# Moving five small transfers ahead of three transposes in a full DMA queue

The change: the transfers that put the last rows of a small matrix M in place go behind the third turned query tile instead of the sixth; the fourth to sixth turned query tiles follow them.

## The chip, the cores and the metric

One core of one Trainium2 chip. The metric is the device time of the whole kernel in microseconds (us).

Engines: PE is TensorE (PEld its weight loads), DVE VectorE, ACT ScalarE, POOL GpSimd, SP SyncE, whose queue SPq issues most of the DMA transfers here (93 of the 117 DMA instructions in the trace of before). All data matrices are bf16.

## The reference, cut to what matters

```python
def _A_ref(x, wqkv, wo):                      # S = 2048, D = 640, 32 heads of 20
    q, k, v = ...                             # from x @ wqkv
    phi = lambda t: jnp.where(t > 0, t + 1, jnp.exp(t)) + 1e-6
    pq, pk = phi(q), phi(k)
    kv = einsum(pk, v); z = sum(pk)
    o = (pq @ kv) / (pq @ z + 1e-6)
    return o @ wo
def _B_ref(x, w1, w2, w3, w4):
    h  = gelu(layernorm(x) @ w1)              # then shifted along the sequence, @ w2
    x1 = x + hs
    return x1 + gelu(layernorm(x1) @ w3) @ w4
return g * A + (1 - g) * B                    # g = sigmoid(x . gate_w)
```

The kernel folds `kv` and `wo` into one 640x640 matrix M, so the attention output of a 128-row tile is (normalized `pq` tile) @ M.

## The kernel before: the parts that matter

A scheduler written in Python orders the whole program when it is built. Work is a set of items; an item is emitted when the items it depends on have been emitted, and that fixes the order of each engine's instructions, with semaphores between engines. So a dependency added to an item can order a queue without any data behind it. The items here:

```python
def m_first():                       # matmuls for most of M; ACT and DVE evict them to M_sb
    ...
def m_tail():                        # item ("mt",): the last rows of M, into rows 60..67 of M_sb
    for j in range(KD):              # KD = 5
        sch.dma("sp", M_sb[60:68, j, :], Mt[8 * j:8 * j + 8, :], "mt", group_total=KD)
def qt_tile(t):                      # item ("qt", t): turn a normalized query tile
    sch.dma("sp", pqnT[:, :, 128 * t:128 * (t + 1)], pq_tok[:, t, :], ..., transpose=True)
def t_xn(which, t):                  # item ("t2", t): turn a layernormed tile
    sch.dma("sp", xnT[:, :, 128 * t:128 * (t + 1)], xn[:, sx, :], ..., transpose=True)
def a_tile(t):                       # item ("a", t): attention output of tile t
    ts(pool, abx[:, sa, :], x_tok[:, t, :], stg[:, 3, t:t + 1], ...)          # GpSimd
    mm_group(..., [(pqnT[:, j, tok], M_sb[:, j, 0:512]) for j in range(KD)])  # PE
    mm_group(..., [(pqnT[:, j, tok], M_sb[:, j, 512:D]) for j in range(KD)])
    stt(abx[:, sa, :], psf[...], stg[:, 2, t:t + 1], abx[:, sa, :], ...)      # DVE evicts
# ... cut ...
IT.add("MT", ("mt",), 0.0, m_tail, deps=[(("m", 1), 1.5), (("qt", 5), 0.0)])
IT.add("T2", ("t2", u), 0.0, lambda u=u: t_xn(2, u), deps=[(("n2", u), 1.1)] + ([(("mt",), 0.0)] if u == 12 else []))
IT.add("QT", ("qt", t), 0.0, lambda t=t: qt_tile(t), deps=[..., (("t2", 11 if t < 6 else NT - 1), 0.0)])
IT.add("AT", ("a", t), 1.33, lambda t=t: a_tile(t), deps=[(("qt", t), 3.0), ..., (("mt",), 2.5), ...])
```

The order on SP is therefore: xn tiles 8 to 11, query tiles 0 to 5, the five M transfers, xn tiles 12 to 15, query tiles 6 on. `xn` has three buffers, so GpSimd cannot normalize tile 15 before tile 12 has been turned. On PE the first attention tiles are interleaved with groups of the W3 matmul: a group, tile 0, a group, tile 1, and so on.

## Time and profile before

| | before |
|---|---|
| median, 3 runs | 262.55 us (262.35 to 262.55) |
| span in the profile | 261.4 us |
| PE busy | 257.3 us, 98% |
| PE wait for the M transfers | 0.78 us in the timeline, about 0.95 us of lost time (below) |

First part of the page of before (engine, busy us, share, instructions):

```profile
span 261.4 us, 4276 instructions
PE 257.3 (98%) x1665; PEld 133.9 (51%) x1665; DVE 151.7 (58%) x289; ACT 112.1 (43%) x241; POOL 93.0 (36%) x152
```

With PE busy for 257.3 of 261.4 us, a change that takes no work away can gain only from a gap on PE. The list of PE's waits in before has three lines (who waited, for whom, us in total, times, longest):

```profile
PE ps L848 <- POOL xn L660: 1.1, 1, 1.1
PE ps L601 <- DMA M_sb<-Mt: 0.8, 1, 0.8
PE ps L875 <- DMA wq<-in_A_wqkv_dram: 0.2, 1, 0.2
```

Only the second lies in the middle of the kernel. The SP queue's timeline around it, before (start us, us, what, count; in brackets idle time and releaser, where there is any):

```profile
120.69 5.79 SPq L281 DMA_TRANSPOSE xnT<-xn  x4
126.53 9.00 SPq L281 DMA_TRANSPOSE pqnT<-pq_tok  x6
135.66 4.13 SPq L285 DMA_DIRECT2D M_sb<-Mt  x5
139.88 5.19 SPq L281 DMA_TRANSPOSE xnT<-xn  x4
145.12 7.89 SPq L281 DMA_TRANSPOSE pqnT<-pq_tok  x6
```

PE's timeline in the same stretch, before:

```profile
126.45 0.74 PE L1006 MATMUL ps<-wo_aug,Lt 60*64 60x512 bf16 x16
127.12 13.12 PE L601 MATMUL ps<-xnT,w 128*128 128x512 bf16 x60
141.03 1.53 PE L601 MATMUL ps<-M_sb,pqnT 128*128 128x512 bf16 x10 [0.78 <-DMA M_sb<-Mt]
```

And the chain that ended last, before, in order of time:

```profile
127.19 10.91 PE ps L601 x50
138.13 0.61 ACT h2T L657
138.73 0.38 SPq L285
139.16 1.81 DMA M_sb<-Mt
141.03 9.92 PE ps L601 x60
```

How to read these: six transposes keep SP's queue until 135.53, the five M transfers are then issued one after the other until 139.79, and 0.06 us after the last of them has landed (139.16 + 1.81 = 140.97) the first attention matmul starts. The issue of the last transfer takes only 0.62 us; the chain counts the landing, 1.81 us after the issue starts. The ACT and SPq pieces of the chain are inferred releasers between the W3 matmuls and the issue; what stood ahead of that issue is read from the queue's own timeline.

Two more lines, GpSimd's and DVE's timelines of before, show what else was late there:

```profile
142.56 0.88 POOL L623 TENSOR_SCALAR xn<-x_tok,st 128x640 bf16<-128x640 bf16 x1 [11.63 <-DMA xnT<-xn]
144.33 0.88 DVE L640 SCALAR_TENSOR_TENSOR abx<-ps,stg,abx 128x640 f32<-128x640 f32 x1 [3.02 <-POOL abx L623]
```

GpSimd waited for xn tile 12 to be turned, and so DVE evicted the first attention tile late.

### The profile page before, as it was taken

The numbers are of one execution on the slowest core, as the hardware profiler recorded it, in microseconds if no ns is written. First come the engines' busy times: TensorE is split into PE (matmuls) and PEld (weight loads), VectorE is DVE, ScalarE is ACT, GpSimd is POOL, SyncE is SP. The second block draws the span as 40 slices with busy tenths as digits, with TensorE's granted clock in tenths as the row PEclk, the third lists the DMA queues.
The fourth block names the chain that finished last, engine by engine and source line by source line (L and its number), as shares of the span: only waits on it lengthen the run. The fifth ranks groups of instructions, "written<-read, shape, count | busy, mean of one in ns | idle before, by whom it ended". The sixth has DMA issues, their size and how long they took to land.

```text
span 261.4 us, 4276 instructions
## 1 busy us (share of the span) xinstructions
PE 257.3 (98%) x1665; PEld 133.9 (51%) x1665; DVE 151.7 (58%) x289; ACT 112.1 (43%) x241; POOL 93.0 (36%) x152
## 2 busy tenths in 40 slices
PE   8999999999999999999998999999999999999996
PEld 4655555554455555554444545654455644455453
DVE  1497787899903799998996406993023320133232
ACT  1386767759355766685853240005500035200000
POOL 4003996869864019667901401130011110021001
DMA  6865869582656991362572670123000020000211
GB/s 196 256 103 143 165 173 171 168 142 42 107 107 125 354 332 31 74 104 51 110 95 58 125 78 0 25 65 113 0 3 0 0 103 0 0 3 1 100 53 50
DMA packets 51348, 24.99 MB, mean 96 GB/s; under 512 B 42708, under 2 KB 49917, under 8 KB 51328
## 3 DMA queue, kind: packets, MB, share of 16 engines
q1 hardware_dynamic: 49952, 21.31, 35.4%
q0 software_dynamic: 1136, 3.28, 5.6%
q8 instruction: 13, 0.21, 0.3%
q10 hardware_dynamic: 240, 0.13, 0.2%
q14 instruction: 7, 0.06, 0.1%
HBM read 12.05 MB, written 2.62 MB: 56 GB/s over the span
## 4 chain that ended last, share of the span: by engine, by line
PE 96%; DMA 2%; SPq 0%; DVE 0%; ACT 0%; issue 0%
PE ps L601 60%; PE ps L1176 22%; PE ps L783 8%; PE ps L875 2%; DMA wq<-in_A_wqkv_dram 1%; PE ps L1088 1%; PE ps L1158 1%; DMA M_sb<-Mt 1%; PE ps L974 1%; PE ps L876 1%; SPq L285 0%; DVE x_tok L640 0%; PE ps L1006 0%; PE ps L612 0%; ACT h2T L657 0%; PE ps L1155 0%
## 5 line engine op out<-in xcount | busy, mean ns | idle before, releaser
L601 PE MATMUL ps<-xnT,w 128*128 128x512 bf16 x360 | 81.6, 379 | 0.0
L657 ACT ACTIVATE h2T<-ps 128x512 bf16<-128x512 f32 x52 | 30.5, 598 | 68.5 <-PE ps L601 68.5
L1176 PE MATMUL ps<-w,h2T 128*128 128x512 bf16 (+1 forms) x416 | 58.8, 299 | 0.0
L601 PEld LDWEIGHTS ps<-xnT,w 128*128 128x128 bf16 x360 | 34.2, 98 | 38.2 <-issue 0.9
L640 DVE SCALAR_TENSOR_TENSOR x_tok<-ps,stg,abx 128x512 bf16<-128x512 f32 (+1 forms) x32 | 17.3, 550 | 61.1 <-PE ps L1176 61.1
L623 POOL TENSOR_SCALAR abx<-x_tok,stg 128x640 f32<-128x640 bf16 x16 | 14.8, 928 | 97.5 <-DVE x_tok L640 94.2
L1176 PEld LDWEIGHTS ps<-w,h2T 128*128 128x128 bf16 x416 | 32.1, 98 | 24.9 <-issue 1.1
L623 POOL TENSOR_SCALAR xn<-x_tok,st 128x640 bf16<-128x640 bf16 x32 | 34.5, 1086 | 17.9 <-DMA xnT<-xn 17.2
L657 ACT ACTIVATE Er<-ps 128x640 bf16<-128x640 f32 x32 | 22.5, 705 | 18.5 <-PE ps L876 8.6
L601 PE MATMUL ps<-M_sb,pqnT 128*128 128x512 bf16 (+1 forms) x160 | 24.4, 299 | 0.8 <-DMA M_sb<-Mt 0.8
L656 ACT ACTIVATE junk<-x_tok 128x640 bf16<-128x640 bf16 x32 | 23.6, 737 | 3.1 <-DVE x_tok L638 2.6
L657 ACT ACTIVATE hsT<-ps 128x512 bf16<-128x512 f32 (+1 forms) x32 | 18.9, 593 | 13.4 <-PE ps L601 13.0
L601 PE MATMUL ps<-w,hsT 128*128 128x512 bf16 (+1 forms) x160 | 23.7, 299 | 0.0
L601 PE MATMUL ps<-wkg,xT 128*128 128x512 bf16 (+1 forms) x150 | 22.6, 299 | 0.0
L640 DVE SCALAR_TENSOR_TENSOR abx<-ps,stg,abx 128x640 f32<-128x640 f32 x16 | 14.1, 884 | 14.4 <-PE ps L601 7.4
L601 PEld LDWEIGHTS ps<-w,hsT 128*128 128x128 bf16 x160 | 13.3, 98 | 12.2
L601 PEld LDWEIGHTS ps<-M_sb,pqnT 128*128 128x128 bf16 x160 | 13.1, 98 | 11.9 <-DMA M_sb<-Mt 1.3
L601 PE MATMUL ps<-wq,xT 128*128 128x512 bf16 (+1 forms) x120 | 18.3, 299 | 0.0
L783 PE MATMUL ps<-pk_tok,x_tok 128*128 128x512 bf16 x80 | 17.8, 379 | 0.0
L623 DVE TENSOR_SCALAR Er<-Er 128x640 bf16<-128x640 bf16 x32 | 11.6, 362 | 9.4 <-ACT Er L657 9.2
L601 PEld LDWEIGHTS ps<-wkg,xT 128*128 128x128 bf16 x150 | 12.2, 97 | 9.0
L638 DVE SCALAR_TENSOR_TENSOR x_tok<-ps,x_tok 128x640 bf16<-128x640 f32 x16 | 13.1, 820 | 6.0 <-PE ps L601 5.1
(76 smaller groups left out, 241.1 us busy)
## 6 DMA issues: line engine op xcount, KB each, us to landing
w<-in_B_w_dram SPq DMA_DIRECT2D x1, 2160.0 KB, 8.2
w<-in_B_w_dram SPq DMA_DIRECT2D x1, 2080.0 KB, 15.1
x_tok<-in_A_x_dram SPq DMA_DIRECT2D x3, 640.0 KB, 5.7
out_dram<-x_tok SPq DMA_DIRECT2D x3, 640.0 KB, 3.1
w<-in_B_w_dram POOLq DMA_DIRECT2D x8, 160.0 KB, 4.4
wq<-in_A_wqkv_dram SPq DMA_DIRECT2D x5, 160.0 KB, 3.9
wkg<-in_A_wqkv_dram SPq DMA_DIRECT2D x5, 160.0 KB, 3.9
wv<-in_A_wqkv_dram POOLq DMA_DIRECT2D x1, 800.0 KB, 6.1
```

The costliest lines, as they stand in the source:

```text
L601: ins = e.matmul(out_ap, l, r, start=(i == 0), stop=(i == n - 1))
L623: return engf(lambda e: e.tensor_scalar(out_ap, in_ap, s1, s2, op0, op1), rd, [out_ap], cost=cost)
L638: return dve(lambda e: e.scalar_tensor_tensor(out_ap, in0, scalar, in1, op0, op1, accum_out=accum), rd, [out_ap, accum], cost=cost + 70.0)
L640: return dve(lambda e: e.scalar_tensor_tensor(out_ap, in0, scalar, in1, op0, op1), rd, [out_ap], cost=cost)
L656: return act(lambda e: e.activation(out_ap, in_ap, func, bias=bias, scale=scale, accum_out=accum), rd, wr, cost=cost)
L657: return act(lambda e: e.activation(out_ap, in_ap, func, bias=bias, scale=scale), rd, wr, cost=cost)
L783: ins = e.matmul(o, l, r, start=(t0 + q_ == 0), stop=(t0 + q_ == NT - 1))
L875: e.matmul(ps[:, b, 0:512], l, w[:, k, 0:512], start=(k == 0), stop=(k == KD - 1))
L876: return e.matmul(ps[:, b + 1, 0:n2], l, w[:, k, 512:512 + n2], start=(k == 0), stop=(k == KD - 1))
L974: ins = e.matmul(o, l, r_, start=st_, stop=sp_, skip_group_check=True)
L1088: ins = e.matmul(o, l, r, start=st, stop=sp)
L1176: ins = e.matmul(o, l, r, start=False, stop=(i == KFF - 1), skip_group_check=(n0 > 0))
```

## The change

Its intent: land the M rows before PE needs them, by letting three of the six query tiles wait behind them.

```diff
-    IT.add("MT", ("mt",), 0.0, m_tail, deps=[(("m", 1), 1.5), (("qt", 5), 0.0)])
+    IT.add("MT", ("mt",), 0.0, m_tail, deps=[(("m", 1), 1.5), (("qt", 2), 0.0)])
@@
-        IT.add("QT", ("qt", t), 0.0, lambda t=t: qt_tile(t), deps=[..., (("t2", 11 if t < 6 else NT - 1), 0.0)])
+        IT.add("QT", ("qt", t), 0.0, lambda t=t: qt_tile(t), deps=[..., (("t2", 11 if t < 6 else NT - 1), 0.0)] + ([(("mt",), 0.0)] if t == 3 else []))
```

More of the change, by code (lines that the diff above doesn't have):

```diff
@@ L1267, in _build @@
         IT.add("QN", ("qn", t), 0.0, lambda t=t: qn_scale(t), [(("qs", t), 0.0)])
-        IT.add("QT", ("qt", t), 0.0, lambda t=t: qt_tile(t), deps=[(("qn", t), 3.2), (("w2", NT - 1), 0.5), (("t2", 11 if t < 6 else NT - 1), 0.0)])
+        IT.add("QT", ("qt", t), 0.0, lambda t=t: qt_tile(t), deps=[(("qn", t), 3.2), (("w2", NT - 1), 0.5), (("t2", 11 if t < 6 else NT - 1), 0.0)] + ([(("mt",), 0.0)] if t == 3 else []))
     for t in range(NT):
```

## The prediction

> **What bounds it now.** TensorE. The page's first part has PE busy for 257.3 of 261.4 us (98%), at full granted clock; the chain that ended last is 96% PE and 2% DMA. [...] The list of waits shows three on PE, two of them at the start. The third is "PE ps <- DMA M_sb<-Mt", once, 0.8 us (1.3 us on the weight load).
>
> **That wait in order of time.** On the SP queue six turned query tiles (pqnT) are issued from 126.53 to 135.53, then the five M_sb<-Mt transfers from 135.66 to 139.79 (0.64 us each to issue), then four turned xn tiles to 145.07. The last M transfer starts at 139.16 and has landed at 140.97; the first attention-output matmul starts at 141.03. The W3 matmul before it started at 139.85 and such matmuls follow each other every 0.216 us (1.08 us for five), so it could have started at about 140.07. Loss: 0.96 us, estimated from these times. After 141.03 the chain is unbroken PE work to 258.7.
>
> **What the change does.** No work is added or removed. The list scheduler fixes the PE order through its dependencies (each of the first attention tiles sits between two fixed W3 groups), so I expect the same PE, ACT and DVE programs and PSUM banks; only the SP queue, and perhaps one GpSimd position, is permuted: three pqnT, five M transfers, the fourth pqnT, then xn tiles 12 to 15 and the last two pqnT in some mixture.
>
> Costed: three transposes at 1.33 us put the first M transfer at 130.5; M_sb is evicted by 129.5, so it need not wait. Five take 4.2 us; the last starts at 134.0 and lands near 135.8. Needed at 140.07: 4 us of slack, where before it was 0.9 us late. The fourth pqnT lands near 138.5, needed at about 146.5. The displaced tiles are issued no later than 145: query tiles 4 and 5 are needed after 158, xn tiles 12 to 15 at about 151. Side effect: GpSimd's last xn tile waited for a transposition until 142.56 and so delayed the first abx tile and DVE's first attention eviction (144.33). If xn tile 12 moves ahead, this shrinks; it cost PE nothing, so it gains nothing.
>
> **On the critical path:** the whole 0.96 us. 262.55 - 0.96 = **261.6 us** (0.37% less), range 261.2 to 262.3. Chances: faster by over 2% 0.01, within 2% 0.98, slower by over 2% 0.01.
>
> **What would show it right or wrong.** Right: no PE wait on M_sb<-Mt; the chain without that DMA; the first M_sb,pqnT matmul near 140.1, the M_sb transfers starting near 130.5; every later PE piece about 0.95 us earlier; span near 260.4. Wrong in the first step: the M transfers still issued after 134. In the second: the stall gone but a new PE wait in the following 15 us, on a PSUM bank held for an abx tile, on pqnT, or on xnT before the half W3 groups. In the third: the pieces start earlier but the end does not.
>
> **What would make it wrong.** A changed PE order or bank choice from the shifted priorities; slower transposes around 130.5 (one of the six took 2.38 us instead of 1.2, a quarter of the slack); scatter between runs, up to 0.3 us. [...]the 1.81 us from issue to landing, shown in the trace, is what gets hidden.

The cuts in it are remarks that no trace of this case shows; no term of the forecast is among them, and its sum stays 262.55 - 0.96 = 261.6 us. Its "full granted clock" is the 1.000 that is listed for the run (a caution on such listings stands under the controls).

## The result, and the profile after

| | before | after |
|---|---|---|
| median of 6 runs | 262.39 us (261.57 to 262.55) | 261.13 us (260.85 to 261.36) |
| ratio of the fast runs | | 0.9955 (95%: 0.994 to 0.9969) |
| span in the profile | 261.4 us | 259.9 us |
| first M product matmul starts | 126.45 us | 125.85 us |
| from there to the first attention matmul | 14.58 us | 13.63 us |
| from the first attention matmul to the end | 120.37 us | 120.42 us |

The instructions of PE, ACT, DVE and GpSimd are the same in the same order (one semaphore wait of DVE stands two places earlier); otherwise only SP's order differs. The page of after, first part:

```profile
span 259.9 us, 4277 instructions
PE 256.2 (99%) x1665; PEld 133.2 (51%) x1665; DVE 152.0 (59%) x289; ACT 112.2 (43%) x241; POOL 92.9 (36%) x152
```

PE's waits, after:

```profile
PE ps L848 <- POOL xn L660: 1.1, 1, 1.1
PE ps L612 <- DMA x_tok<-in_A_x_dram: 0.3, 1, 0.3
PE ps L875 <- DVE xT L666: 0.2, 1, 0.2
```

The wait for M_sb<-Mt is gone, and no other wait of the middle took its place; what is left lies in the first 7 us. SP's queue, after:

```profile
125.92 3.93 SPq L281 DMA_TRANSPOSE pqnT<-pq_tok  x3
129.95 4.37 SPq L285 DMA_DIRECT2D M_sb<-Mt  x5
134.77 1.23 SPq L281 DMA_TRANSPOSE pqnT<-pq_tok  x1
136.11 3.85 SPq L281 DMA_TRANSPOSE xnT<-xn  x3
140.01 2.60 SPq L281 DMA_TRANSPOSE pqnT<-pq_tok  x2
142.71 1.22 SPq L281 DMA_TRANSPOSE xnT<-xn  x1
```

The scheduler did more than the diff says: three xn tiles passed two query tiles. In before, query tiles 4 and 5 were urgent because M, and through it attention tile 0, stood behind them; now they are not, and the xn tiles rank higher. PE's timeline and the chain that ended last, after:

```profile
126.52 13.12 PE L601 MATMUL ps<-xnT,w 128*128 128x512 bf16 x60
139.48 1.52 PE L601 MATMUL ps<-M_sb,pqnT 128*128 128x512 bf16 x10
```

```profile
126.59 22.81 PE ps L601 x120
149.40 2.28 PE ps L1088 x20
```

One unbroken piece of PE work runs now from 126.59 to 149.40. GpSimd and DVE, after:

```profile
138.80 0.88 POOL L623 TENSOR_SCALAR xn<-x_tok,st 128x640 bf16<-128x640 bf16 x1 [8.49 <-DMA xnT<-xn]
141.19 0.88 DVE L640 SCALAR_TENSOR_TENSOR abx<-ps,stg,abx 128x640 f32<-128x640 f32 x1
```

The two profiles differ by 1.5 us, and the last three rows of the table split that: 0.60 us arose before the first M product matmul (the first of `m_first`, PE's L1006; six matmuls for the rest of M run near 94 us and are not meant here), up to which both programs are the same, 0.95 us between it and the first attention matmul, and nothing after that. Whether the 0.60 us belongs to the change had to be tried.

### The profile page after: what moved, and what is told of

It reads as the page before. It is cut to its first block, busy times and chain, and to the rows that moved or that the text cites. A ratio compares the mean times of both kernels' runs of the same rounds, so it can differ in the third digit from the quotient of the medians.

```text
span 259.9 us, 4277 instructions
## 1 busy us (share of the span) xinstructions
PE 256.2 (99%) x1665; PEld 133.2 (51%) x1665; DVE 152.0 (59%) x289; ACT 112.2 (43%) x241; POOL 92.9 (36%) x152
## 3 DMA queue, kind: packets, MB, share of 16 engines
HBM read 12.05 MB, written 2.62 MB: 56 GB/s over the span
## 4 chain that ended last, share of the span: by engine, by line
PE 97%; DMA 2%; SPq 0%; DVE 0%; issue 0%
PE ps L601 61%; PE ps L1176 22%; PE ps L783 8%; PE ps L875 2%; DMA x_tok<-in_A_x_dram 2%; PE ps L1088 1%; PE ps L1158 1%; PE ps L974 1%; PE ps L876 1%; SPq L285 0%; DVE x_tok L640 0%; PE ps L1006 0%; PE ps L612 0%; PE ps L1155 0%
## 5 line engine op out<-in xcount | busy, mean ns | idle before, releaser
L1117 DVE TENSOR_TENSOR pq_tok<-pq_tok,dnr 128x300 bf16<-128x300 bf16 (+1 forms) x48 | 16.4, 395 | 0.6
```

The source lines that it names most:

```text
L1117: dve(lambda e, o=o, i0=i0, i1=i1: e.tensor_tensor(o, i0, i1, ALU.mult), [i0, dnr[:, 1, sd, :]], [o], cost=cost)
```

## The experiments

Theory A: PE waits for the landing of the last M transfer, and only the time at which that lands counts. Rival B: xn tile 12 moving ahead, which frees GpSimd and DVE, makes the gain. Theory C, for the excess: a part of the difference between profiles is start-up scatter. Rival D: the gain needs the transfers well ahead. Twelve runs were made, all with correct results: eight new kernels, and the kernels before and after twice each.

The diffs below are shortened to the item and its dependencies. The measure used throughout is taken from each profile, free of the start-up: from the first M product matmul to the first attention matmul (13.63 us without a wait).

### Controls: the kernel before, twice, and the changed kernel, twice

Edit: none.

> The kernel before, unchanged, as a control. Three theories are tried in these runs. A (mine): the gain is the wait of TensorE for the last of the five M_sb<-Mt transfers, 0.96 us, and only the place of these transfers in the SP queue matters. B (rival): the gain comes from xn tile 12 moving ahead in the same queue, which frees GpSimd and DVE for the first attention tile earlier. C (rival, for a part): 0.60 us of the 1.5 us between the two profiles arose in the first 14 us, before anything that was changed[...]. All theories: ratio 1.000 within 0.002; one wait for M_sb<-Mt of 0.8 us on TensorE; from the first M product matmul (126.45 us in the profile of before) to the end of the span 134.95 us, within 0.15. C also expects the start of that matmul to differ between profiles of the same kernel by several tenths of a us.

> The changed kernel, unchanged. A and B: ratio to before about 0.9963 (0.96 us), from the first M product matmul to the end 134.05 us within 0.15, no TensorE wait on M_sb<-Mt. C: the ratio of these runs may lie anywhere from 0.994 to 0.998, and its start-up part differs from the earlier profile's.

> The kernel before once more, for its start-up. C (start-up scatter): the first M product matmul starts anywhere between 125.6 and 127.3 us, as it did in ten profiles of kernels with the same first 126 us. If the start-up belongs to the kernel's text: 126.45 to 126.51, as in both earlier profiles of it. From that matmul to the first attention matmul 14.58 us in either case.

> The changed kernel once more, for its start-up. C: the first M product matmul starts anywhere between 125.6 and 127.3 us. If the start-up belongs to the kernel's text: 125.85 to 125.89. 13.63 us from there to the first attention matmul in either case.

null_before: median 262.62 us against 262.27 for the kernel before in the same rounds, ratio 1.0011 (0.9997 to 1.0024); 14.57 us. after_again: 261.16 us, ratio 0.9961 (0.9948 to 0.9974); 13.63 us. null_third and after_third (one time each, on another chip): 262.12 and 261.40 us; 14.32 and 13.63 us.

The first M product matmul started at 126.51 (null_before), 125.89 (after_again), 126.15 (null_third) and 126.14 us (after_third). Until the third pair this looked as if the start-up belonged to the kernel's text, since the first two pairs agreed (126.45 and 126.51 against 125.85 and 125.89). On that other chip the two kernels start alike. All 14 profiles, whose programs are the same up to there, lie between 125.66 and 127.32 us, and xn_only, which keeps the wait, starts at 126.03 us. So the 0.60 us are scatter as far as these profiles show, and C holds. PE's timelines of before and of after show a piece of it, the first query matmul:

```profile
5.42 0.61 PE L875 MATMUL ps<-wq,xT 128*128 128x512 bf16 x1 [0.24 <-DMA wq<-in_A_wqkv_dram]
```

```profile
5.11 0.38 PE L875 MATMUL ps<-wq,xT 128*128 128x512 bf16 x1 [0.21 <-DVE xT L666]
```

In before it still takes 0.61 us (and a second one at 6.14 takes 0.63), in after 0.38 us. The clock records kept in the traces bear on this. Eight of the 14 traces say when the clock first became full: from 4.26 us (split, whose first M product matmul is the earliest, 125.66) to 6.98 us (behind_seven, the latest, 127.32). In behind_seven the matmuls of this form at 5.11 and 5.80 us, before its full clock, take 0.59 and 0.63 us; in after, whose record of the full clock begins at 4.47 us, those at 5.11 and 5.49 us take 0.38 us. But m_first, with 4.56 us, starts its first M product at 126.57; its list of PE's waits has one of 0.8 us in the start-up, for nothing that the profile shows. So the clock is one source of the scatter in these traces and not the only one; waits for the first loads (0.2 to 0.6 us for wq) may be another, and they were not separated.

A caution for reading clocks: the other six traces, that of before among them, hold no clock record, and such a run is listed with a clock of 1.000 although the matmul above took 0.61 us. So a listed 1.000 says here only that no fall was recorded.

null_third's own wait was 0.5 us in the list instead of 0.8: the size of the wait varies by itself, by how fast the queue ahead of it runs (its six query tiles took 8.74 us, not 9.00).

### m_only and xn_only: the two halves of what happened to the queue

m_only moves the M transfers but keeps xn tile 12 behind the sixth query tile:

```diff
# against the changed kernel
-  ("t2", u): deps=[(("n2", u), 1.1)] + ([(("mt",), 0.0)] if u == 12 else [])
+  ("t2", u): deps=[(("n2", u), 1.1)] + ([(("qt", 5), 0.0)] if u == 12 else [])
```

xn_only lets xn tile 12 change places with the sixth query tile and keeps six transposes ahead of M:

```diff
# against the kernel before
-  ("mt",):   deps=[(("m", 1), 1.5), (("qt", 5), 0.0)]
+  ("mt",):   deps=[(("m", 1), 1.5), (("t2", 12), 0.0)]
-  ("t2", u): ... + ([(("mt",), 0.0)] if u == 12 else [])
+  ("t2", u): ... + ([(("qt", 4), 0.0)] if u == 12 else [(("mt",), 0.0)] if u == 13 else [])
-  ("qt", t): ...
+  ("qt", t): ... + ([(("mt",), 0.0)] if t == 5 else [])
```

> The M transfers behind the third turned query tile, but xn tiles 12 to 15 left behind the sixth, where before has them. A: no TensorE wait on M_sb<-Mt, the full gain: ratio 0.9963, 134.05 us from the first M product matmul to the end; GpSimd's last xn tile still waits until about 142 and DVE's first attention eviction stays near 143 to 144.5. B: no gain, ratio 1.000, 134.95 us, as GpSimd and DVE stay late.

> xn tile 12 changes places with the sixth turned query tile, so that six transposes still stand before the M transfers. A: the wait stays, 0.8 us in the list of waits, ratio 1.000, 134.95 us from the first M product matmul to the end, although GpSimd's last xn tile is done by about 139.5 and DVE evicts the first attention tile about 1.8 us sooner than before. B: the gain, ratio 0.9963, 134.05 us.

m_only: median 261.59 us, ratio 0.9972 (0.996 to 0.9984), 13.63 us, no PE wait for M. GpSimd and DVE stayed late, as these lines of its timelines show:

```profile
141.76 0.87 POOL L623 TENSOR_SCALAR xn<-x_tok,st 128x640 bf16<-128x640 bf16 x1 [11.29 <-DMA xnT<-xn]
143.52 0.88 DVE L640 SCALAR_TENSOR_TENSOR abx<-ps,stg,abx 128x640 f32<-128x640 f32 x1 [2.67 <-POOL abx L623]
```

xn_only: median 262.51 us, ratio 1.0007 (0.9993 to 1.0022), 14.77 us. Its wait in the list, and the same two lines:

```profile
PE ps L601 <- DMA M_sb<-Mt: 1.0, 1, 1.0
```

```profile
136.77 1.50 POOL L623 TENSOR_SCALAR xn<-x_tok,st 128x640 bf16<-128x640 bf16 x1 [6.28 <-DMA xnT<-xn]
142.37 0.88 DVE L640 SCALAR_TENSOR_TENSOR abx<-ps,stg,abx 128x640 f32<-128x640 f32 x1 [0.98 <-PE ps L601]
```

Here GpSimd and DVE are freed, and nothing is gained. B is out: M early with xn late gives the gain, xn early with M late does not. The wait came out 0.19 us longer than in before because the queue ahead took that much longer (12.83 us from the first query tile to the last M transfer, against 12.63).

### behind_fifth, behind_seven and m_first: how early is early enough

```diff
# behind_fifth, against the changed kernel
-  ("mt",): deps=[(("m", 1), 1.5), (("qt", 2), 0.0)]       ("qt", 3) waits for ("mt",)
+  ("mt",): deps=[(("m", 1), 1.5), (("qt", 4), 0.0)]       ("qt", 5) waits for ("mt",)
# behind_seven, against the kernel before
-  ("mt",): deps=[(("m", 1), 1.5), (("qt", 5), 0.0)]       ("t2", 12) waits for ("mt",)
+  ("mt",): deps=[(("m", 1), 1.5), (("t2", 12), 0.0)]      ("t2", 12) waits for ("qt", 5), ("t2", 13) for ("mt",)
# m_first, against the changed kernel
-  ("mt",): deps=[(("m", 1), 1.5), (("qt", 2), 0.0)]       ("qt", 3) waits for ("mt",)
+  ("mt",): deps=[(("m", 1), 1.5)]                         ("qt", 0) waits for ("mt",)
```

> The M transfers behind the fifth turned query tile, one transpose less than before. Theory A (TensorE waits for the landing of the last M transfer, which moves with the number of transposes ahead of it): one transpose less is 1.3 us, against a wait of 0.96 us, so the wait is just gone: the last transfer lands at about 139.7, 0.3 us before its need; 134.05 us from the first M product matmul to the end (0.1 more at most), ratio about 0.9963 to 0.997. A rival D, that the gain needs the transfers to be well ahead, for instance because the transposes and the small transfers disturb each other: a wait of several tenths of a us stays, or the tail is over 134.4.

> The M transfers behind one transpose more than before (xn tile 12 goes ahead of them, the rest of the order as before). A: the wait grows by that transpose, 1.3 us: about 2.1 us in the list of waits instead of 0.8, 136.25 us from the first M product matmul to the end, ratio 1.005. B, for which xn tile 12 moving ahead is what gains: ratio at or below 1.000.

> The M transfers ahead of all turned query tiles; SP then waits for the eviction of M until about 129.3, and every transpose after them is later (the first query tile issued near 133.7 instead of 126). DVE evicts M one item earlier too. A: the last transfer lands near 135, the first query tile near 136.4, both before 139.5: no new TensorE wait, tail 134.05 us, ratio 0.9963, the same as the change; earlier than needed gains nothing more. D: less gain, as the transposes are delayed by some 3.5 us, or a TensorE wait on pqnT or xnT appears.

behind_fifth: median 261.23 us, ratio 0.9962 (0.9937 to 0.9987), 13.63 us. One transpose less ahead is already enough: the last M transfer was issued at 137.38, and 1.87 us later is 139.25, 0.35 us before the first attention matmul at 139.60.

m_first: 13.63 us and no wait, so no better than the change, as A has it. The median is 261.79 us and the ratio 1.000 (0.9957 to 1.0042), which misses the expected 0.9963. One run of 265.15 us, at full clock, is in that ratio; the other five have a mean of 261.69 us against 262.29 for before, 0.9977. Its profile has the same 134.03 us from the first M product matmul to the end as the change, with a late start-up (126.57). What the 265.15 us run did is not known.

behind_seven: median 264.03 us, ratio 1.0076 (1.0034 to 1.0118), 15.92 us. The wait grew by 1.34 us, one transpose, as expected; its ratio was higher than the expected 1.005, which its interval still holds. PE's timeline, and the time by stretches (us, then busy time of PE, PEld, DVE, ACT, POOL with counts, the granted clock, the DMA share, GB/s):

```profile
143.24 2.62 PE L601 MATMUL ps<-M_sb,pqnT 128*128 128x512 bf16 x10 [2.13 <-DMA M_sb<-Mt]
```

```profile
143.00:143.50 0.50, 0.26 (x2) 0.14 (x3) 0.00 (x0) 0.00 (x0) 0.00 (x0) 1.00 0.33 70
143.50:144.00 0.50, 0.50 (x3) 0.22 (x2) 0.00 (x0) 0.00 (x0) 0.00 (x0) 0.52 1.10 218
144.00:145.00 1.00, 1.00 (x4) 0.30 (x2) 0.00 (x0) 0.00 (x0) 0.00 (x0) 0.50 0.47 93
147.00:148.00 1.00, 1.00 (x6) 0.43 (x5) 0.00 (x0) 0.43 (x1) 0.67 (x1) 1.00 0.75 149
```

After the wait the granted clock is 0.50; the trace's clock record says for 3.413 us. Ten attention matmuls take 2.62 us instead of 1.52, and the rest of the kernel from the first attention matmul takes 122.06 us instead of 120.40. Two of the six runs had it (clock 0.994 on average; 266.56 and 265.09 us), four did not (1.000; mean 263.49 us, 1.2 us over before). The mean of all six carries both.

### behind_nine: a longer wait, for the clock

```diff
# against the kernel before
-  ("mt",): deps=[(("m", 1), 1.5), (("qt", 5), 0.0)]       ("t2", 12) waits for ("mt",)
+  ("mt",): deps=[(("m", 1), 1.5), (("t2", 14), 0.0)]      ("t2", 12) waits for ("qt", 5), ("t2", 15) for ("mt",)
```

> The M transfers behind six turned query tiles and three xn tiles. The run behind_seven showed a wait of 2.13 us and after it a granted TensorE clock of 0.5 for 3.41 us, so that the part after the wait took 122.06 instead of 120.40 us. Theory E: a wait of TensorE long enough makes its clock fall to half for one such stretch, which adds about 1.66 us to the wait. By A the wait here grows by three transposes of 1.3 us over before: from the first M product matmul to the first attention matmul 18.5 us (13.63 without a wait, 14.58 in before). By E the part after it takes about 122.06 us in the profile, and the ratio is near 1.021 (3.9 us of wait and 1.7 us of clock more than before, whose 0.95 us wait showed no fall of the clock). Without E (the fall in behind_seven was chance): 120.4 us and a ratio near 1.015.

Median 268.15 us, ratio 1.0226 (1.0208 to 1.0245); 18.52 us from the first M product matmul to the first attention matmul, as forecast. PE's timeline:

```profile
144.44 2.85 PE L601 MATMUL ps<-M_sb,pqnT 128*128 128x512 bf16 x10 [4.72 <-DMA M_sb<-Mt]
```

The clock fell in all four runs: to 0.987 on average in three, 0.994 in one. In the profile it is at half for 6.827 us (141.76 to 148.59), part of which lies inside the wait, and the part after the wait takes 122.46 us, 2.06 us more than at full clock, where 1.66 was expected. These lines of the time by stretches show the fall and the return:

```profile
140.00:142.00 2.00, 0.00 (x0) 0.00 (x0) 1.23 (x4) 0.35 (x1) 0.00 (x0) 0.94 0.13 23
148.00:150.00 2.00, 2.00 (x10) 0.83 (x9) 0.21 (x1) 0.60 (x1) 0.79 (x1) 0.85 0.51 102
```

Theory E (a long enough wait makes the clock fall) fits these runs: the clock fell in all four of the kernel with the wait of 4.72 us, while no fall was recorded in the 33 runs of before beside the experiments (in the profiles of before the wait is 0.5 to 0.8 us). 3.94 us of added wait and 2.06 us of lost clock make 6.0 us, and the measured ratio is worth 5.9 us (0.0226 of 262.1). The clock records put the fall at 143.51 us in behind_seven, 2.40 us after its wait began (141.11), and at 141.76 us in behind_nine, 2.04 us after its wait began (139.72). For the four runs of behind_seven without a fall no trace was kept, so what sets them apart from the other two is not shown.

### split: three transfers early, two late

```diff
# against the kernel before
-    def m_tail():
-        for j in range(KD):
+    def m_tail(j0, j1):
+        for j in range(j0, j1):
-  ("mt",):  m_tail,                 deps=[(("m", 1), 1.5), (("qt", 5), 0.0)]
+  ("mta",): lambda: m_tail(0, 3),   deps=[(("m", 1), 1.5), (("qt", 2), 0.0)]     # ("qt", 3) waits for it
+  ("mt",):  lambda: m_tail(3, KD),  deps=[(("m", 1), 1.5), (("qt", 5), 0.0)]
```

> Three of the five M transfers behind the third turned query tile, two left behind the sixth. A: the first attention tile needs all five, and the last of them has the same work ahead of it in the queue as before, so the wait stays: 0.8 us in the list of waits, tail 134.95 us, ratio 1.000. If the number of transfers that are early counted, some three fifths of the gain: ratio 0.998.

A miss for what I wrote under A: I had the wait unchanged, and it fell to about 0.3 us (13.94 us). Median 261.99 us, ratio 0.9979 (0.9953 to 1.0005; one run of 265.25 us at clock 0.994 counts as slow and is left out). The end of the chain, split:

```profile
126.40 13.06 PE ps L601 x60
139.46 0.14 issue
139.60 5.47 PE ps L601 x32
```

The reason is in the queue, not in PE. The same eleven items ahead of and including the last M transfer took less: its issue started 11.86 us after the first query tile (125.75 to 137.61), against 12.63 us in before (126.53 to 139.16). In before the fourth query tile took 2.38 us instead of 1.28; in split the slow moment fell on the third M transfer, which took 1.03 us instead of 0.67. The first attention matmul still came 1.99 us after the issue of the last M transfer. The trace has that transfer landed at 139.51 us, and the weight load for the first attention matmul at 139.56 us after 0.60 us of idle time, though the list of PE's waits names no M transfer. So the rule of A stands and my estimate of the queue was off. By the time alone, this run cannot tell A from a gain in proportion to the number of early transfers; the rule below can.

### pool_queue: the same transfers from another queue

```diff
-            sch.dma("sp", M_sb[60:68, j, :], Mt[8 * j:8 * j + 8, :], "mt", group_total=KD)
+            sch.dma("pool", M_sb[60:68, j, :], Mt[8 * j:8 * j + 8, :], "mt", group_total=KD)
```

> The five M transfers issued by GpSimd, in its order after the third of its last four xn tiles, instead of by SP, whose order is else that of before. A: what counts is when the last lands, not the order on SP; GpSimd is free from about 130.9, and its loads of similar size took 4.1 us from issue to landing in the profile of before, so the last lands between 135 and 140, where 139.6 is needed: the wait is gone or under 0.4 us, 13.6 to 14.0 us from the first M product matmul to the first attention matmul, ratio 0.996 to 0.998. If the gain were tied to SP's order of transposes: no gain, 14.58 us.

Median 261.41 us, ratio 0.9966 (0.9949 to 0.9983), 13.63 us, no wait. SP's order of transposes is that of before, so the gain isn't tied to it. GpSimd's timeline:

```profile
130.63 2.63 POOL L285 DMA_DIRECT2D M_sb<-Mt  x5
```

Five issues took 2.63 us and the landing a median of 2.4 us, not the 4.1 us I had taken from GpSimd's weight loads, which are not of similar size as I wrote but four times larger (40 KB against 10 KB); the result does not depend on that.

### All profiles in one table

| kernel | last M transfer issued (us) | first attention matmul (us) | later by | M product to attention | wait in PE's list |
|---|---|---|---|---|---|
| behind_nine | 142.57 | 144.44 | 1.87 | 18.52 | 4.7 |
| behind_seven | 141.38 | 143.24 | 1.86 | 15.92 | 2.1 |
| xn_only | 138.94 | 140.80 | 1.86 | 14.77 | 1.0 |
| before | 139.16 | 141.03 | 1.87 | 14.58 | 0.8 |
| null_before | 139.21 | 141.08 | 1.87 | 14.57 | 0.8 |
| null_third | 138.60 | 140.47 | 1.87 | 14.32 | 0.5 |
| split | 137.61 | 139.60 | 1.99 | 13.94 | none listed |
| behind_fifth | 137.38 | 139.60 | 2.22 | 13.63 | none |
| m_only | 134.02 | 139.63 | 5.61 | 13.63 | none |
| after_third | 133.96 | 139.77 | 5.81 | 13.63 | none |
| after_again | 133.73 | 139.52 | 5.79 | 13.63 | none |
| after | 133.70 | 139.48 | 5.78 | 13.63 | none |
| m_first | 132.66 | 140.20 | 7.54 | 13.63 | none |

(pool_queue, not issued by SP, also has 13.63 and no wait.)

The first attention matmul starts at the later of two times: 13.63 us after the first M product matmul, when PE has done the work before it, or 1.86 to 1.99 us after the issue of the last M transfer. That is theory A in one sentence, over waits from 0 to 4.7 us. D is out by behind_fifth, whose PE timeline has no wait here:

```profile
139.60 1.52 PE L601 MATMUL ps<-M_sb,pqnT 128*128 128x512 bf16 x10
```

## Why the prediction was right

- **The step costed, 0.96 us of PE wait.** Right. 14.58 fell to 13.63 us, 0.95 us, in the first pair of profiles, and 14.57 to 13.63 in the second; m_only and xn_only show that the M transfers alone do it.
- **Same PE, ACT and DVE programs.** Right: only SP's order differs. GpSimd's, which the text left open ("perhaps one GpSimd position"), is the same too; xn tile 15 is only done earlier in time.
- **When the transfers start and land.** Predicted 130.5 for the first and 134.0 for the last. Measured 129.95 and 133.70 in a profile that runs 0.60 us earlier there, so 130.55 and 134.30 on the clock of before. The third of them took 1.30 us instead of 0.67; this is the slow moment that the prediction named, and it ate 0.6 of about 4 us of slack.
- **Nothing gives the gain back.** Right: 120.37 and 120.42 us from the first attention matmul to the end, and all later PE pieces stand 1.55 us earlier, of which 0.95 is the change.
- **The freed GpSimd and DVE gain nothing.** Right, by xn_only.
- **The time.** Forecast 261.6, range 261.2 to 262.3; the median came out at 261.13, 0.07 us below the lower end. The difference of the means of the same rounds is 1.19 us (262.30 to 261.10) against 0.96. The repeat (after_again) gave 0.9961, 1.0 us. The mechanism and the size of its term are right. What was mis-sized is the scatter ("scatter between runs, up to 0.3 us"): start-ups of the same program lay up to 1.7 us apart between profiles (125.66 to 127.32), the control null_before differed from before by 0.3 us in the mean without any change, and the runs of before in the second group ranged from 261.13 to 263.36 us.

What stays open: whether the packet of an instruction queue that goes along with the slow DMA work near 131 us in each of these kernels is its cause (last section), and what the single runs of 265.15 us (m_first, full clock) and 265.25 us (split, clock 0.994) did. No experiment beats the changed kernel beyond scatter; m_only, behind_fifth and pool_queue end at the same 13.63 us, since the wait can only be taken away once.

## What to carry to other kernels

When PE waits for a small transfer, look at what stands ahead of its *last* piece in its own queue: moving it in front of transposes that are needed later was worth the wait here (0.95 us) and no more, and going further ahead than enough brought nothing. Check the gain inside the profile, between two instructions on either side of the wait, because start-up scatter (1.7 us between the profiles here) can be larger than an effect of 0.4%. Reckon that a PE wait can cost more than itself: in the kernel with a wait of 2.13 us the clock fell in two of six runs and cost 1.66 us in the profile, in the one with 4.7 us it fell in all four and cost 2.06 us.

## What else the traces show

- The clock after a short wait. A wait of 2.13 us (behind_seven) was followed by half clock in the profile, for 3.413 us, and two of six runs of that kernel had a reduced mean clock (0.994); with a wait of 4.7 us (behind_nine) all four runs had it (0.987 or 0.994). In all 33 runs of before beside the experiments no fall was recorded (clock 1.000); the wait in its profiles is 0.5 to 0.8 us. One run of split doesn't fit in: its mean clock was 0.994, though the wait in split's profile is only 0.3 us; its cause is not known. The clock fell 0.27 us after PE had resumed in behind_seven (143.24 to 143.51 us), and inside the wait in behind_nine (141.76 us, PE resumed at 144.44). What sets the moment of the fall was not shown.
- What it cost to stand behind others in a queue. Here each 128x640 transpose ahead cost 1.3 us of issue (1.22 to 1.29 each for the six ahead of M in before but for the slow one, and the gap), and a 10 KB transfer 0.62 to 0.79 us but for slow ones, with 1.87 us from the last issue to the first use.
- A slow moment of the DMA engines near 131 us. In the profile of before, by stretches, the times of the DMA packets add up to more than the engines' full time while little is moved:

```profile
130.00:131.00 1.00, 1.00 (x6) 0.43 (x5) 0.93 (x3) 0.72 (x2) 0.92 (x2) 1.00 0.90 121
131.00:132.00 1.00, 1.00 (x6) 0.49 (x5) 1.00 (x4) 0.52 (x2) 0.00 (x0) 1.00 1.52 27
```

  The last two columns are the DMA share and GB/s: 1.52 with 27 GB/s, against 0.90 with 121 a microsecond earlier. The item issued then took longer than its like by 0.4 us (split, an M transfer), 0.6 us (after, an M transfer) or 1.1 us (before, a transpose). The traces show what goes along with it: in each of the 14, one 16 KB packet of the queue that the profile page lists as "q8 instruction" starts between 129.71 and 131.40 us and takes 0.88 to 1.61 us; the slow item overlaps it or follows within 0.4 us (in before the packet runs from 130.54 to 131.82 us and the slow transpose from 130.51 to 132.89 us). The same holds in the whole kernel: of the 840 turned x, xn and query tiles in the 14 traces, 717 overlap no packet of the instruction queues (q8 and q14) and take at most 1.41 us, while all 50 that take over 1.45 us lie among the 123 that overlap one. No experiment moved these packets, so that they are the cause is not shown.
